# Cosine attention and a highway layer on one core: k of three batches and x of the last one transposed by DMA, another end for the last two tiles

## The chip, the cores and the metric

The kernel runs on one core of one Trainium2 chip. The metric is the device time of one execution in microseconds (us); several executions are timed and the median is given. A profile is one more execution, recorded by the hardware profiler: it has a time of its own, and a span from the first to the last instruction of the program. The engines are TensorE (PE; its weight loads are PEld), VectorE (DVE), ScalarE (ACT), GpSimd (POOL) and SyncE (SP). Each runs its own queue of instructions in order and waits for others on semaphores.

## The reference

```
q, k, v: (8, 12, 448, 64) float32;  tau = 0.1;  w_h, w_t: (768, 768);  b_t: (768)

q_n = q / (norm(q, axis=-1) + 1e-6);   k_n = k / (norm(k, axis=-1) + 1e-6)
attn = softmax(q_n @ k_n.T / tau)                      # per batch and head, 448 x 448
x = (attn @ v), heads side by side                     # (8 * 448, 768)

H = maximum(x @ w_h, 0)
T = 1 / (1 + exp(-(x @ w_t + b_t)))
out = T * H + (1 - T) * x                              # (3584, 768) float32
```

## The kernel before

The eight batches go through three parts: normalising and transposing q and k, attention, and the highway layer (the code calls it ffn). The parts of several batches overlap in time. Twelve heads make six pairs, and two pairs make a group, so each batch has three groups g. A sequence of 448 is split into 64 rows l of 7 columns j. A q or k tile has two halves of 64 partitions, one for the even and one for the odd heads; an x tile has two such halves for two neighbouring columns j.

*Normalising.* `norm` squares a group of q or k (`sq`, on ScalarE; L377) and VectorE sums it (`rd`, L385). `newton` on VectorE makes the inverse root y for batches 1 to 7; `lnexp` on ScalarE does it for batch 0. `scale` multiplies by y into the fp16 tiles qn and kn (L425), on GpSimd but for a part of batch 0. kn has eight columns: seven and one that a shift leaves half empty and that is set to zero.

*Transposing.* `turn` makes qT and kT. On TensorE that is seven or eight transposes against an identity (L442) into PSUM, and a copy by VectorE (`cpq`, `cpk`; L450). For q of batches 3 to 7 (QDMA) it is one transposing DMA from SyncE's queue instead (`xd7`, L444). x of batches 1 to 6 (XDMA) goes the same way (`xd6`, and `xd3` for the short last tile of a batch; L648); x of batches 0 and 7 by TensorE (`xt6`, `xt3`; L644) and a copy (`cpx`, L654).

*Attention.* Scores are products of K = 64 in the two row halves of the array at once (`qk`, L484; `qkt`, L495), ScalarE makes their exponentials (L490, L497), products with v follow (`av`, L509 and L514; `avt`, in column halves, L522), and VectorE divides by the sums (`rc`, `ev`; L529, L530) into x.

*The highway layer.* A batch has four tiles, numbered 4 b + i: three of 768 columns and a short one of 384 (i = 3). So tiles 28 to 31 are those of the last batch. A tile's product with w_t (wi = 0) and with w_h (wi = 1) comes in halves of 384 columns, each issued as two groups of three products (L668). The short tile's go in pairs to the two column halves of the array (L665). After w_t: z = P + bias (`za`, DVE, L677), tanh on ScalarE (`th`, L684), T = 0.5 tanh + 0.5 (`gt`, DVE, L686). After w_h: hm = max(P, 0) - x (`hm`, DVE, L680), hm = T * hm (`gg`, DVE, L689), os = x + hm (`out`, on GpSimd; on VectorE for tiles 30 and 31, L694). Two DMAs from SyncE's queue store the two partition halves (`st`; L701 for short tiles, L704 for the others).

What sets the order of everything: each operation is recorded with what it reads and writes, and ORDER, a list written into the kernel, gives the order in which they are issued, SLOTS which buffer of its ring each one takes (eight banks of PSUM, three kn, four kT, four os and so on). An operation whose name is in PORT keeps GpSimd's next such instruction behind the VectorE one that is recorded ahead of it. Wherever the array changes between whole (F), two row halves (T) and two column halves (C), the operations' mode changes.

Around the change, q's transposing DMA stands in `turn` like this:

```
if nm == "q" and b in QDMA:
    op("SP", f"xd7 {b} {g}", lambda: nc.sync.dma_start(
        R("qT", i)..., R("qn", i)..., transpose=True), r=[("qn", i, 0), ("qn", i, 1)], w=[tn(nm, i)])
    return
```

Of the kernel before, what the change touches and what calls it, by code (L numbers as in the profile page):

```python
# [12 lines left out]
ALU = mybir.AluOpType  # L13
# [78 lines left out]
""".split()  # L92
)

SLOTS = {
    "qr": "01010101",
    "kr": "0120121",
    "kn": "012012012012102021210210",
    "vr": "01001010",
    "vp": "01010101",  # L100
    "sq": "012012012120120120120121201201012210210122202101",
    "n2": "01010101",
    "y": "01201201",
    "tu": "01010101010",
# [93 lines left out]
def kernel(  # L198
# [11 lines left out]
    nc = tc.nc  # L210
# [3 lines left out]
    CC = DM // 128  # L214
# [591 lines left out]
```

## Time and profile before

| | |
|---|---|
| median of 3 runs | 257.26 us (257.17 to 257.95) |
| profiled execution | 256.1 us, span 254.3 us |
| granted TensorE clock, mean | 0.968 |
| busy: PE, DVE, ACT, POOL | 236.7, 210.6, 214.6, 170.2 us |
| DMA queue q1 (SyncE's), share of the 16 engines | 51.7% |
| DMA queue q0 (GpSimd's), share of the 16 engines | 36.7% |

A busy time is the time in which an engine had an instruction under way. TensorE's products overlap, so their pace is read from the distance between starts. In a group's line the part ahead of the bar names the line of the program, the engine, the operation, its tiles and shapes and the count; behind it stand the busy time, the mean of one in ns, the idle time just before such instructions, and what ended it. In the chain of the work that ended last, each line has a start, a length and what ran.

### The profile page before, as it was taken

Reading aid. Unit: us, or ns where it says so; the run is one execution under the profiler, and the core shown is the slowest. Engines: PE = TensorE matmul, PEld = TensorE weight load, DVE = VectorE, ACT = ScalarE, POOL = GpSimd, SP = SyncE. Lnnn points to the kernel's source line nnn. Section 1 sums busy time; section 2 is a strip of 40 time slices with the busy share of each in tenths; the row PEclk is TensorE's granted clock in tenths of the full one; section 3 lists DMA queues with packets and bytes.
Section 4 is the critical chain, followed back from the end, with each engine's and each line's share of the span. In section 5 each row is a group of like instructions: output and inputs, shape, how many; then the busy total and the mean of one; then the engine's idle time right before and its main releaser. Section 6 shows DMA issues by size and latency. Waiting matters only on the chain.

```text
span 254.3 us, 7465 instructions
## 1 busy us (share of the span) xinstructions
PE 236.7 (93%) x2937; PEld 150.3 (59%) x2937; DVE 210.6 (83%) x471; ACT 214.6 (84%) x425; POOL 170.2 (67%) x210
## 2 busy tenths in 40 slices
PE   8376999999999999999999999999999999999980
PEld 2156776566656675566575665656556755667640
DVE  4887797897999999989997789989986763868893
ACT  2688999999999999999999999999968997591210
POOL 5478366956978696689879965687737784142440
PEclk9756999999999999999999999999999999999998
DMA  7999999999599995899999999995792065407175
GB/s 225 284 223 207 270 266 239 146 145 292 81 141 327 177 148 110 167 296 169 185 144 198 307 159 153 163 342 108 146 214 65 3 136 107 129 0 189 22 213 139
DMA packets 63283, 44.72 MB, mean 176 GB/s; under 512 B 38928, under 2 KB 60048, under 8 KB 63248
## 3 DMA queue, kind: packets, MB, share of 16 engines
q1 hardware_dynamic: 43120, 31.11, 51.7%
q0 software_dynamic: 19856, 12.68, 36.7%
q8 instruction: 23, 0.38, 0.6%
q10 hardware_dynamic: 272, 0.46, 0.5%
q14 instruction: 12, 0.10, 0.1%
HBM read 38.34 MB, written 11.01 MB: 194 GB/s over the span
## 4 chain that ended last, share of the span: by engine, by line
PE 78%; ACT 9%; DVE 5%; DMA 3%; POOL 1%; issue 1%; SPq 0%; DVEq 0%; ACTq 0%
PE B L668 34%; PE B L484 11%; PE B L514 9%; PE B L665 5%; PE B L442 5%; PE B L509 4%; ACT E L490 3%; DMA qr<-in_q_dram 3%; PE B L522 3%; PE B L495 3%; ACT sq L377 3%; ACT E L574 2%; PE B L561 2%; PE B L588 1%; POOL kn L425 1%
## 5 line engine op out<-in xcount | busy, mean ns | idle before, releaser
L490 ACT ACTIVATE E<-B 128x448 f16<-128x448 f32 x252 | 125.2, 640 | 7.5 <-PE B L484 6.7
L668 PEld LDWEIGHTS <-xT 128*128 128x128 f16 x576 | 52.6, 98 | 37.9 <-issue 6.7
L694 POOL TENSOR_TENSOR os<-x,hm 128x384 f32<-128x384 f16 x53 | 47.5, 917 | 30.0 <-DVE hm L689 23.6
L425 POOL TENSOR_TENSOR qn<-qr,y 128x448 f16<-128x448 f32 x47 | 43.2, 932 | 26.1 <-DVE qn L425 5.7
L668 PE MATMUL B<-wh,xT 128*128 128x384 f16 x288 | 57.0, 326 | 0.1
L668 PE MATMUL B<-wt,xT 128*128 128x384 f16 x288 | 55.6, 326 | 0.1
L385 DVE TENSOR_REDUCE n<-sq 128x14 f32<-128x896 f32 (+1 forms) x50 | 51.1, 1037 | 1.8 <-ACT sq L377 1.8
L425 POOL TENSOR_TENSOR kn<-kr,y 128x448 f16<-128x448 f16 x42 | 39.0, 943 | 7.8 <-DVE vp L456 3.9
L684 ACT ACTIVATE tt<-z 128x768 f16<-128x768 f32 (+1 forms) x32 | 25.8, 835 | 17.3 <-DVE z L677 17.3
L514 PE MATMUL B<-vp,E 128*128 128x65 f16 x756 | 37.6, 193 | 0.0
L484 PE MATMUL B<-qT,kT 64*128 64x448 f16 x252 | 35.1, 353 | 0.1
L514 PEld LDWEIGHTS <-E 128*128 128x128 f16 x756 | 33.4, 97 | 2.3
L677 DVE TENSOR_TENSOR z<-B,bias 128x384 f32<-128x384 f32 x48 | 25.5, 550 | 10.1 <-PE B L668 9.0
L680 DVE SCALAR_TENSOR_TENSOR hm<-B,x 128x384 f16<-128x384 f32 x56 | 30.2, 548 | 3.0 <-PE B L668 1.7
L509 PE MATMUL B<-vp,Et 128*128 128x130 f16 x126 | 28.1, 223 | 0.0
L497 ACT ACTIVATE Et<-B 128x448 f16<-128x448 f32 x42 | 26.8, 650 | 0.4
L530 DVE SCALAR_TENSOR_TENSOR x<-B,rd 128x448 f16<-128x448 f32 x42 | 25.6, 616 | 0.7
L377 ACT ACTIVATE sq<-qr 128x896 f32<-128x896 f32 (+1 forms) x24 | 24.5, 1036 | 0.6 <-DMA qr<-in_q_dram 0.6
L377 ACT ACTIVATE sq<-kr 128x896 f32<-128x896 f16 x21 | 22.2, 1075 | 0.8 <-DMA kr<-in_k_dram 0.8
L335 POOL DMA_DIRECT2D vr<-in_v_dram x32 | 21.7, 683 | 0.7 <-DVE vp L456 0.7
L574 ACT ACTIVATE E<-B 128x384 f16<-128x384 f32 (+1 forms) x42 | 21.3, 636 | 0.9 <-PE B L561 0.6
L450 DVE COPY kT<-B 128x1024 f16<-128x1024 f16 x23 | 15.7, 681 | 4.0 <-PE B L442 2.0
(72 smaller groups left out, 305.2 us busy)
## 6 DMA issues: line engine op xcount, KB each, us to landing
out_dram<-os SPq DMA_DIRECT2D x48, 192.0 KB, 3.3
qr<-in_q_dram SPq DMA_DIRECT2D x6, 1344.0 KB, 8.5
kr<-in_k_dram POOLq DMA_DIRECT2D x7, 672.0 KB, 9.9
vr<-in_v_dram POOLq DMA_DIRECT2D x16, 192.0 KB, 8.0
qr<-in_q_dram SPq DMA_DIRECT2D x6, 448.0 KB, 7.4
vr<-in_v_dram POOLq DMA_DIRECT2D x16, 144.0 KB, 6.4
out_dram<-os SPq DMA_DIRECT2D x16, 96.0 KB, 3.4
wt<-in_moe_w_t_dram POOLq DMA_DIRECT2D x1, 1152.0 KB, 13.2
```

The source lines that it names most:

```text
L377: nc.scalar.activation(dst, src, AF.Square, scale=sc)
L385: nc.vector.reduce_sum(R("n2", b)[:, c : c + 7 * n], a, axis=AX.X)
L425: ENG[eng].tensor_mul(R(nm + "n", i)[:, o : o + NJ, t, :], source(nm, b, g)[:, t].rearrange("l (j d) -> l j d", d=D), R("y", b)[:, c : c + ...
L484: nc.tensor.matmul(R("B", ("S", n, c, t))[:, 0:S], lhsT=R("kT", i)[ln, s, 128 * c : 128 * c + 128], rhs=queries(ln), start=True, stop=True)
L490: nc.scalar.activation(R("E", n)[:, at : at + 7, :].rearrange("l j x -> l (j x)"), R("B", ("S", n, c, t))[:, 0:S], AF.Exp)
L497: op("ACT", f"expt {n}", lambda: nc.scalar.activation(R("Et", n).rearrange("l j x -> l (j x)"), R("B", ("St", n))[:, 0:S], AF.Exp), r=[("B ...
L509: nc.tensor.matmul(U[:, 2 * c : 2 * c + 2, :], lhsT=Et[:, 2 * c : 2 * c + 2, :].rearrange("l j x -> l (j x)"), rhs=vp[:, 6:8, 0:65], start ...
L514: nc.tensor.matmul(U[:, 2 * c + t, :], lhsT=E[:, at : at + 2, :].rearrange("l j x -> l (j x)"), rhs=vp[:, 3 * t + m, 0:65], start=False, s ...
L574: op("ACT", f"ex{m} {n}", lambda X=X, m=m, t=t, o=o: nc.scalar.activation(flat()[:, o + 512 * t : o + 512 * t + m], R("B", X)[:, 0:m], AF. ...
L668: nc.tensor.matmul(P[:, 0:MH], lhsT=xT[:, cc, :], rhs=w_[:, cc, MH * mh : MH * mh + MH], start=(cc == 0), stop=(cc == CC - 1))
L680: op("DVE", f"hm {g} {mh}", lambda at=at, sl=sl, mh=mh: nc.vector.scalar_tensor_tensor(out=R("hm", g)[:, sl], in0=R("B", at)[:, 0:MH], sca ...
L694: op(eng, f"out {g} {mh}", lambda sl=sl, mh=mh: ENG[eng].tensor_add(R("os", g)[:, sl], xpart(mh), R("hm", g)[:, sl]), r=[("gg", g), xk], w ...
```

## The change

k of batches 5 to 7 (KDMA) is transposed by two DMAs for each group, one for each half of the partitions, from SyncE's queue (`xdk`). So that their blocks land in order, kn is laid out with every other column, each scaling of k becomes two instructions (four and three columns; `kn4`, `kn3`), and the loads and copies of v follow the same order of columns. x of batch 7 is transposed by DMA as well. The squares of k, group 1, of batches 2 to 5 (SQP) move from ScalarE to GpSimd.

The last two tiles (30 and 31; NLATE) are combined in another form. With T known, VectorE makes `cx`: os = (T - 1) * x. Behind each product with w_h come two operations: `hg`: hm = max(P, 0) * T, and `ou`: os = hm - os. For tile 31 the product with w_h goes in two halves of 192 columns to each column half of the array (`fth`), with its `hg3` and `ou3`. The two stores of these tiles go one from SyncE's queue and one from ScalarE's (`sl6`, `sl3`).

ORDER and SLOTS are written anew throughout.

```diff
-    XDMA, QDMA = range(1, B - 1), range(3, B)
+    XDMA, QDMA, KDMA = range(1, B), range(3, B), range(5, B)
+    SQP = tuple(("k", b, 1) for b in range(2, 6))
...
-        engs = SPLIT.get(i, (("DVE" if i in SQV else "ACT"),))
+        engs = SPLIT.get(i, (("DVE" if i in SQV else "POOL" if i in SQP else "ACT"),))
...
+                elif eng == "POOL":
+                    nc.gpsimd.tensor_mul(dst, src, src)
...
     def scale(nm, b, g, engs):
+            for lo, hi in ((0, 7),) if nm == "q" else ((0, 4 - t), (4 - t, 7)):
...
+                        N[:, :, t, :] if nm == "q" else N[:, lo > 0 : (lo > 0) + 2 * (hi - lo) - 1 : 2, t, :],
...
+        if nm == "k" and b in KDMA:
+            for s in range(2):
+                op("SP", f"xdk {b} {g} {s}", lambda s=s: nc.sync.dma_start(
+                    R("kT", i)[:, s, :].rearrange("p (j x) -> p j x", j=8),
+                    R("kn", i)[64 * s : 64 * s + 64].rearrange("l j t d -> l (j t d)"), transpose=True),
+                   r=[("kn", i, 0), ("kn", i, 1), ("zkn",)], w=[tn(nm, i)])
+            return
...
+        late, last = g >= 4 * B - NLATE, g == 4 * B - 1
...
+                if last and wi:
+                    for n in range(2):
...
+                                    c0 = MH * h + MH // 2 * n
+                                    nc.tensor.matmul(P[64 * h : 64 * h + 64, 0 : MH // 2], lhsT=xT[:, cc % 3, 64 * (cc // 3) : 64 * (cc // 3) + 64],
+                                                     rhs=w_[:, cc, c0 : c0 + MH // 2], start=(cc == 0), stop=(cc == CC - 1))
+                        op("PE", f"fth {g} {n}", half, r=[("xT", g), (wn,)], w=[("B", at)], mode="C")
...
+                        op("DVE", f"hg3 {g} {n}", ...scalar=0.0, in1=R("tt", g)[:, sl], op0=ALU.max, op1=ALU.mult),
+                        op("DVE", f"ou3 {g} {n}", ...nc.vector.tensor_sub(R("os", g)[:, sl], R("hm", g)[:, sl], R("os", g)[:, sl]),
...
+                elif late:
+                    op("DVE", f"hg6 {g} {mh}", ...
+                    op("DVE", f"ou6 {g} {mh}", ...
...
+                        op("DVE", f"cx {g} {n}", ...
+                            out=R("os", g)[:, sl], in0=R("tt", g)[:, sl], scalar=-1.0, in1=xpart(n), op0=ALU.add, op1=ALU.mult),
...
+        if late:
+            for h in range(2):
...
+                    eng = (nc.sync, nc.scalar)[h]
...
+                op(("SP", "ACT")[h], f"sl{nb} {g} {h}", put, r=[("os", g)], w=[("o", g, h)])
+            return
```

More of the change, by code (lines that the diff above doesn't have):

```diff
@@ L97 @@
     "kr": "0120121",
-    "kn": "012012012012102021210210",
-    "vr": "01001010",
+    "kn": "012012012012021021021012",
+    "vr": "01010101",
     "vp": "01010101",
-    "sq": "012012012120120120120121201201012210210122202101",
+    "sq": "012012010101201201201201021021021021201021102102",
     "n2": "01010101",
@@ L104 @@
     "tu": "01010101010",
-    "qn": "012012012012021201210210",
-    "qT": "01230123012301230123012",
-    "kT": "01230123013201320132013",
-    "E": "012010201201021010210210120120210210120120210210102102120",
-    "Et": "012102102101201210210210210201012021021210",
-    "rd": "010101010011010101010101010010101101010101010101010101",
-    "x": "012012012",
-    "xT": "01234012340213402310423014230412",
-    "z": "01101010100110010101101001000101",
-    "tt": "01101010011010101010101101101010",
@@ L115 @@
-    "hm": "01202012021201202001212021021021",
-    "os": "01230321203231013013021231203203",
-    "B": (
-        "0123456701234567012345671203614352007630156421653024160426350160234156043217654306512307641275463170"
-        "2546124367012537251057634274637201437062453061546271345062746107346072436571407534605271237605471653"
-        "7401236752413051742035674235106754602713052614702673147635213502460321745027453721430672415360716025"
-        "4137621407125674305407625137052467235603715263056173546025170435170674021573620417023641536071357260"
-        "4137462607143561253047216032761043540261573163025743674567234627154360714635703612465143670135740126"
-        "0371564301324725706354016713402613527041052361703214065324710"
+    "qn": "012012022102021021021021",
@@ new lines @@
+    "qT": "01230123102102312032103",
+    "kT": "01230123012301230123012",
+    "E": "012012021021021222012012021021201201201201201012020102102",
+    "Et": "012102102102102101210212102012102101210210",
+    "rd": "011011010101101010100101010101010101010101010101010101",
+    "x": "012012012",
+    "xT": "01234021342014302130410234210421",
+    "z": "01011001011010001000010110101010",
+    "tt": "01010110101010101010101110001010",
+    "hm": "01220210021020120210012001200120",
+    "os": "01231023123023110310310120310312",
@@ new lines @@
+    "B": (
+        "0123456701234567012345670213467061532462153476240157632570624153027162504327142657302716034152467102"
+        "4720634173254176403576415260432560142357160257460271506432051643125076314203762041374631206340517513"
+        "7062451034761520461752473105632046715647120531620451745612034572067153047125671230751671045276342510"
+        "7364203643571640745127364072534126526317431720657124035617204637156243574023157413054267126012735607"
+        "1243726410746513240175026731426036752314057126540372612075163471760542310521705632147627305641203675"
+        "2106312745603217561437021547502631407263517420631"
@@ L124 @@
     ),
 }
-PORT = ("nt", "gt", "gg", "vc", "qn", "kn", "vt", "out")
+PORT = ("nt", "gt", "gg", "vc", "qn", "kn", "vt", "out", "cx", "ou")
 class Op:
@@ L216 @@
     NC, NJ = 3, 7
-    WARM, NF = 18, 0
-    XDMA, QDMA = range(1, B - 1), range(3, B)
+    WARM, NF, NLATE = 18, 0, 2
+    XDMA, QDMA, KDMA = range(1, B), range(3, B), range(5, B)
     GROUPS = ((0, 1), (1, 2), (2, 3)), ((0, 1), (1, 3)), ((0, 3),)
@@ L293 @@
     for i, t in enumerate(TILES["kn"]):
-        op("DVE", f"zkn {i}", zero("DVE", [(t[:, 0, 1, :], 0.0), (t[:, 7, 0, :], 0.0)]), w=[("zkn",)])
+        op("DVE", f"zkn {i}", zero("DVE", [(t[:, 6, 1, :], 0.0), (t[:, 7, 0, :], 0.0)]), w=[("zkn",)])
     op("DVE", "zw", zero("DVE", [(wz[:, :], 0.0), (eps[:, :], 1e-14)]), w=[("wz",), ("eps",)])
@@ L333, in fn @@
             def fn(t=t, jj=jj, j0=j0, n=n):
-                c = 64 if (t, jj) == (0, 1) else 0
-                nc.gpsimd.dma_start(R("vr", b)[64 * jj : 64 * jj + 64, 6 * t : 6 * t + 6, c : c + 64 * n].rearrange("l h (c d) -> l h c d", c=n),
+                nc.gpsimd.dma_start(R("vr", b)[64 * jj : 64 * jj + 64, 6 * t : 6 * t + 6, 0 : 64 * n].rearrange("l h (c d) -> l h c d", c=n),
                                     v_src(b)[:, 6 * t : 6 * t + 6, j0 : j0 + n, :])
@@ L377, in fn @@
                     nc.scalar.activation(dst, src, AF.Square, scale=sc)
+                elif eng == "POOL":
+                    assert sc == 1.0
+                    nc.gpsimd.tensor_mul(dst, src, src)
                 else:
@@ L421, in scale, with fn @@
         for t, eng in enumerate(engs):
-            def fn(t=t, eng=eng):
-                c = col(nm, g) + 7 * t
-                o = t if nm == "k" else 0
-                ENG[eng].tensor_mul(
-                    R(nm + "n", i)[:, o : o + NJ, t, :],
-                    source(nm, b, g)[:, t].rearrange("l (j d) -> l j d", d=D),
-                    R("y", b)[:, c : c + 7].unsqueeze(2).to_broadcast([128, NJ, D]))
-            op(eng, f"{nm}n {b} {g} {t}", fn, r=[token(nm, b, g), ("y", b, nm, g)], w=[(nm + "n", i, t)])
+            for lo, hi in ((0, 7),) if nm == "q" else ((0, 4 - t), (4 - t, 7)):
+                def fn(t=t, eng=eng, lo=lo, hi=hi):
+                    c = col(nm, g) + 7 * t
+                    N = R(nm + "n", i)
+                    ENG[eng].tensor_mul(
+                        N[:, :, t, :] if nm == "q" else N[:, lo > 0 : (lo > 0) + 2 * (hi - lo) - 1 : 2, t, :],
+                        source(nm, b, g)[:, t, 64 * lo : 64 * hi].rearrange("l (j d) -> l j d", d=D),
+                        R("y", b)[:, c + lo : c + hi].unsqueeze(2).to_broadcast([128, hi - lo, D]))
+                op(eng, f"{nm}n{hi - lo} {b} {g} {t}", fn, r=[token(nm, b, g), ("y", b, nm, g)], w=[(nm + "n", i, t)])
     def turn(nm, b, g):
@@ L439, in fn @@
             for j in range(nj):
-                to = j if nm == "q" else 2 * ((j - 1) % 3) + (j - 1) // 3 if 0 < j < 7 else 6 + (j == 7)
-                nc.tensor.transpose(T[:, to], R(nm + "n", i)[:, j].rearrange("l t d -> l (t d)"), ident[:, :])
+                nc.tensor.transpose(T[:, j], R(nm + "n", i)[:, j].rearrange("l t d -> l (t d)"), ident[:, :])
         if nm == "q" and b in QDMA:
@@ L457, in fn @@
                     R("vp", b)[:, p0:p1, 3 * t : 3 * t + 3, 0:D],
-                    R("vr", b)[:, 6 * t + p0 : 6 * t + p1, 64 - 64 * t : 256 - 64 * t].rearrange("l p (c d) -> l p c d", c=NC))
+                    R("vr", b)[:, 6 * t + p0 : 6 * t + p1, 0:192].rearrange("l p (c d) -> l p c d", c=NC))
             op("DVE", f"vc{p1 - p0} {b} {p0} {t}", fn, r=[("vr", b, t, 0), ("vr", b, t, 1), ("zvp",)],
@@ L465, in fn @@
                 ln = slice(64 * t, 64 * t + 64)
-                ENG[eng].tensor_copy(R("vp", b)[ln, :, 6 + t, 0:D], R("vr", b)[ln, 6 * t : 6 * t + 6, 192 * t : 192 * t + 64])
+                ENG[eng].tensor_copy(R("vp", b)[ln, :, 6 + t, 0:D], R("vr", b)[ln, 6 * t : 6 * t + 6, 192:256])
             op(eng, f"vt {b} {t}", fn, r=[("vr", b, t, t), ("zvp",)], w=[("vp", b, 6)])
@@ L669, in mm, with half @@
                                              start=(cc == 0), stop=(cc == CC - 1))
+                if last and wi:
+                    for n in range(2):
+                        at = ("P", g, wi, n)
+                        def half(n=n, at=at, w_=w_):
+                            P, xT = R("B", at), R("xT", g)
+                            for cc in range(CC):
+                                for h in range(2):
[3 more added lines that the diff above has]
+                        op("PE", f"fth {g} {n}", half, r=[("xT", g), (wn,)], w=[("B", at)], mode="C")
+                        sl = slice(MH // 2 * n, MH // 2 * n + MH // 2)
+                        op("DVE", f"hg3 {g} {n}", lambda at=at, sl=sl: nc.vector.scalar_tensor_tensor(
+                            out=R("hm", g)[:, sl], in0=R("B", at)[:, 0 : MH // 2], scalar=0.0, in1=R("tt", g)[:, sl], op0=ALU.max, op1=ALU.mult),
+                           r=[("B", at), ("gt", g)], w=[("hm", g, n)], u=[("tt", g)])
+                        op("DVE", f"ou3 {g} {n}", lambda sl=sl: nc.vector.tensor_sub(R("os", g)[:, sl], R("hm", g)[:, sl], R("os", g)[:, sl]),
+                           r=[("hm", g, n), ("cx", g)], w=[("os", g)], u=[("hm", g)])
+                    continue
                 for lo in (0, 3):
@@ L678, in ffn @@
                         R("z", g)[:, sl], R("B", at)[:, 0:MH], biast[:, :] if tail else bias[:, sl]), r=[("B", at), ("b",)], w=[("z", g)])
+                elif late:
+                    op("DVE", f"hg6 {g} {mh}", lambda at=at, sl=sl: nc.vector.scalar_tensor_tensor(
+                        out=R("hm", g)[:, sl], in0=R("B", at)[:, 0:MH], scalar=0.0, in1=R("tt", g)[:, sl], op0=ALU.max, op1=ALU.mult),
+                       r=[("B", at), ("gt", g)], w=[("hm", g, mh)], u=[("tt", g)])
+                    op("DVE", f"ou6 {g} {mh}", lambda sl=sl: nc.vector.tensor_sub(R("os", g)[:, sl], R("hm", g)[:, sl], R("os", g)[:, sl]),
+                       r=[("hm", g, mh), ("cx", g)], w=[("os", g)], u=[("hm", g)])
                 else:
@@ L688, in ffn, with put @@
                    r=[("tt", g)], w=[("gt", g)], u=[("tt", g)])
+                if late:
+                    for n in range(nb // 3):
+                        sl = slice(MH * n, MH * n + MH)
+                        op("DVE", f"cx {g} {n}", lambda sl=sl, n=n: nc.vector.scalar_tensor_tensor(
+                            out=R("os", g)[:, sl], in0=R("tt", g)[:, sl], scalar=-1.0, in1=xpart(n), op0=ALU.add, op1=ALU.mult),
+                           r=[("gt", g), xk], w=[("cx", g)], u=[("tt", g), ("os", g)])
+        if late:
+            for h in range(2):
+                def put(h=h):
+                    rows, O = out[b * S : b * S + S].rearrange("(l j) m -> j l m", j=NJ), R("os", g)[64 * h : 64 * h + 64]
+                    eng = (nc.sync, nc.scalar)[h]
+                    if tail:
+                        eng.dma_start(rows[6, :, MH * h : MH * h + MH], O[:, 0:MH])
+                    else:
+                        eng.dma_start(rows[2 * i + h], O[:, :])
+                op(("SP", "ACT")[h], f"sl{nb} {g} {h}", put, r=[("os", g)], w=[("o", g, h)])
+            return
         op("DVE", f"gg{nb} {g}", lambda: nc.vector.tensor_mul(R("hm", g)[:, 0:W], R("tt", g)[:, 0:W], R("hm", g)[:, 0:W]),
            r=[("gt", g), ("hm", g)], w=[("gg", g)], u=[("tt", g), ("hm", g)])
-        eng = "DVE" if b == B - 1 and i >= 2 else "POOL"
+        eng = "DVE" if g >= 4 * B - 2 else "POOL"
         for mh in range(1 if tail else 2):
```

144 rows, old and new, of the table ORDER are left out of this document.

## The prediction

> **What bounds the kernel now.** I read the page first, then stretches of time, then the chain that ended last, then single groups. Page, busy time and chain by engine:
>
> ```profile
> span 254.3 us, 7465 instructions
> PE 236.7 (93%) x2937; PEld 150.3 (59%) x2937; DVE 210.6 (83%) x471; ACT 214.6 (84%) x425; POOL 170.2 (67%) x210
> PE 78%; ACT 9%; DVE 5%; DMA 3%; POOL 1%; issue 1%; SPq 0%; DVEq 0%; ACTq 0%
> ```
>
> TensorE leads, but a busy TensorE is not one at its peak, so I ask each stage who is idle:
>
> ```profile
> core 0: us, PE busy (x) PEld busy (x) DVE busy (x) ACT busy (x) POOL busy (x), PEclk, DMA share, GB/s
> 0.00:20.00 20.00, 12.62 (x77) 6.87 (x78) 15.00 (x35) 12.50 (x23) 12.06 (x21) 0.74 1.04 244
> 40.00:60.00 20.00, 19.53 (x275) 11.81 (x272) 18.24 (x42) 20.00 (x41) 14.45 (x19) 1.00 1.13 191
> 160.00:180.00 20.00, 20.00 (x279) 12.73 (x273) 17.71 (x41) 19.44 (x39) 14.13 (x17) 1.00 1.01 196
> 180.00:200.00 20.00, 20.00 (x234) 12.21 (x234) 16.01 (x39) 16.59 (x36) 12.71 (x16) 1.00 0.55 126
> 241.50:254.30 12.80, 5.50 (x46) 3.13 (x43) 8.50 (x17) 1.36 (x2) 3.17 (x4) 0.90 0.68 176
> 28.00:247.00 219.00, 218.22 (x2761) 138.26 (x2759) 186.41 (x415) 194.46 (x390) 152.75 (x183) 1.00 0.88 168
> ```
>
> There are three stages. Up to 28 us data are still arriving and TensorE has holes. From 28 to 247 us it is busy in 218.22 of 219 us. From 247 us it has nothing left, and VectorE and the stores finish. ScalarE has no idle time from 40 to 60 us either, so it stands close behind. The pace inside the middle stage is in the chain (start, length, what):
>
> ```profile
> 107.98 0.45 PE B L442 x8
> 123.52 0.67 PE B L484 x6
> 124.19 1.08 PE B L668 x6
> 125.72 0.97 PE B L668 x6
> 219.90 0.19 PE B L484 x2
> 232.39 0.84 PE B L644 x15
> 233.22 8.30 PE B L668 x51
> ```
>
> Fifty-one products at L668 in 8.30 us are 0.163 us each, back to back: this stage has no wait to remove, only work. Work taken from TensorE here shortens the end one for one, if nothing new makes it wait. One more price stands here: six score products (three pairs) would need 3 x 0.19 = 0.57 us and take 0.67, and the six L668 products behind them take 1.08 us where others take 0.97. Each change of the array's shape (whole, two row halves, two column halves) costs 0.10 us.
>
> **The change, part by part.**
>
> *k of batches 5 to 7.* Nine groups lose eight transposes each on TensorE: 9 x 0.45 = 4.05 us, all in the middle stage. VectorE loses their nine copies. SyncE gains 18 transposing DMAs of half the partitions each. The rows:
>
> ```profile
> L450 DVE COPY kT<-B 128x1024 f16<-128x1024 f16 x23 | 15.7, 681 | 4.0 <-PE B L442 2.0 <-PE B L567 1.5 <-ACT E L490 0.5
> L648 SPq DMA_TRANSPOSE xT<-x x24: 1206/1242/2117, 67.9 to 210.5; - x24
>   PEld L668: 0.9, 3
> DMA to landing us min/median/max: 2.3/2.8/9.8
> L444 SPq DMA_TRANSPOSE qT<-qn x15: 1221/1233/1585, 88.6 to 213.8; - x15
> DMA to landing us min/median/max: 2.9/4.1/7.2
> ```
>
> The nine copies are 9 x 0.68 = 6.1 us of VectorE, worth nothing here because it isn't the bound. A transposing DMA holds SyncE's queue 1.24 us, so the 18, with four new ones for x, hold it 22 x 1.24 = 27 us more. Each waits there for both halves of its normalised k from GpSimd, and stores, x and q transposes stand behind it. What hides the landing is distance: I added up, at the paces of this trace, the TensorE work that the new order puts between the last of a group's three DMAs (two k, one q) and the first product that reads them. For the nine groups it is 6.8, 6.4, 8.9, 5.6, 7.0, 4.3, 8.2, 5.7 and 6.1 us. A landing of 4.1 us (the median of the q rows, nearest in source and size) fits under all nine, so I take 0. The bounds are 0 and, with the slowest q landing of 7.2 us in every group, 0.4 + 0.8 + 1.6 + 0.2 + 2.9 + 1.5 + 1.1 = 8.5 us lost.
>
> *x of the last batch.* 15 transposes take 0.84 us, so 21 take 1.18 us, all on TensorE's path. In their place the first DMA must land before tile 28 starts.
>
> ```profile
> L529 DVE RECIPROCAL rd<-B 128x7 f32<-128x7 f32 x42 | 8.3, 200 | 8.3 <-PE B L522 4.9 <-PE B L514 1.7 <-ACT Et L497 1.3
> L530 DVE SCALAR_TENSOR_TENSOR x<-B,rd 128x448 f16<-128x448 f32 x42 | 25.6, 616 | 0.7
> ```
>
> Behind the last attention product the new order holds ten half-groups of three products or pairs, 10 x 3 x 0.163 = 4.9 us. Reciprocal and division take 0.2 + 0.6 us of it, and x lands 2.8 us after its issue: 3.6 against 4.9. So 0; without that cover it costs up to 2.8 us once. The second tile is needed 3.4 us after the first and issued 1.24 us later.
>
> *Changes of shape.* Counted in the order of TensorE's instructions: 163 before, 172 after; 9 x 0.10 = +0.9 us.
>
> *The end.* Rows of the last microseconds and of VectorE's prices:
>
> ```profile
> 245.85 1.14 PE L665 MATMUL B<-wh,xT 128*64 128x384 f16 x12
> 247.56 1.02 DVE L694 TENSOR_TENSOR os<-x,hm 128x384 f32<-128x384 f16 x2
> 248.96 0.25 DVE L686 TENSOR_SCALAR tt<-tt 128x384 f16<-128x384 f16 x1
> 249.64 0.56 DVE L694 TENSOR_TENSOR os<-x,hm 128x384 f32<-128x384 f16 x1
> 250.22 1.11 SPq L701 DMA_DIRECT2D out_dram<-os  x2
> L595 DVE SCALAR_TENSOR_TENSOR x<-B,rd 128x256 f16<-128x256 f32 x9 | 3.6, 417 | 0.1
> L617 DVE SCALAR_TENSOR_TENSOR x<-B,rd 128x128 f16<-128x128 f32 x3 | 0.8, 288 | 0.1
> L689 DVE TENSOR_TENSOR hm<-tt,hm x32: 342/549/809, 53.0 to 249.2; 128x768 f16<-128x768 f16 x24, 128x384 f16<-128x384 f16 x8
> ```
>
> Before: products end at 246.99, VectorE at 250.20, 3.2 us later; it is VectorE's backlog that ends last, not a dependence. After: behind tile 30's last products stand only two halves of tile 31, together as long as the twelve at L665 (six pairs, 6 x 0.163 = 0.98 us). So 0.98 us ahead of the last product's end tile 30 is done, and from there VectorE has hg6, ou6, gt3, ou6, hg3, cx, hg3, ou3, ou3. A 384-wide one follows the next at 0.47 us (two in 1.02), gt3 takes 0.25, and a 192-wide one, between 288 and 417 ns, follows at some 0.3. Sum: 4 x 0.47 + 0.25 + 4 x 0.3 + 0.05 for the last one's end = 3.4, so 2.4 us behind the last product. GpSimd's two adds of tile 29 run beside this. In this trace such a VectorE product took 549 ns at the median and 809 at most, so I add 0.3: 2.7, a gain of 0.5 us (bounds: 0.95, if there is no backlog, and 3.2, as now: a gain of 2.2 or 0). The Trainium skill, "SBUF — State Buffer", section "Who interferes with whom", would have an operation with two SBUF inputs blocked for the whole of GpSimd's; that is one add of 0.9 us, 0.6 more than I take, and the sum below would be -4.4.
>
> The stores: two issues on one queue take 1.11 us; on two queues one goes beside the other, so 0.55 us less (bounds 0 and 0.6; 0 if the two transfers follow each other). End: -0.5 - 0.55 = -1.05. The Trainium skill, "DMA: Bandwidth & Descriptors", section "Rules for kernel authors", advises against two transfers to disjoint partition halves, from two engines as well, because they serialise. By it the second queue brings nothing, and the sum would be -4.45; no run so far shows two such stores from two queues.
>
> *Squares and splits.* Four squares of k move from ScalarE to GpSimd, and each scaling of k there becomes two instructions:
>
> ```profile
> L377 ACT ACTIVATE sq<-kr 128x896 f32<-128x896 f16 x21 | 22.2, 1075 | 0.8 <-DMA kr<-in_k_dram 0.8
> L425 POOL TENSOR_TENSOR kn<-kr,y 128x448 f16<-128x448 f16 x42 | 39.0, 943 | 7.8 <-DVE vp L456 3.9 <-DVE y L403 2.4 <-DVE rd L616 0.6
> L694 POOL TENSOR_TENSOR os<-x,hm 128x384 f32<-128x384 f16 x53 | 47.5, 917 | 30.0 <-DVE hm L689 23.6 <-DVE hm L680 2.9 <-DMA out_dram<-os 1.7
> L787 POOL MEMSET const-float32-0.0<- 128x1 f32 x1 | 0.1, 98 | 0.2 <-issue 0.2
> ```
>
> ScalarE loses 4 x 1.08 = 4.3 us, which it needs to lose: it has no idle time to keep up with a shorter TensorE. GpSimd gains 4 x 2 x 0.94 = 7.5 us and 47 more instructions at about 0.1 (an almost empty one takes 98 ns), 4.7 us; its idle time of 30.0 us ahead of the adds alone covers both. Cost 0; if GpSimd were late, k would be, and that is the late rival below.
>
> *The opening.* GpSimd now issues two loads of v and the whole of wt ahead of its first product, and that product stands behind a second scaling on VectorE.
>
> ```profile
> vr<-in_v_dram POOLq DMA_DIRECT2D x16, 192.0 KB, 8.0
> vr<-in_v_dram POOLq DMA_DIRECT2D x16, 144.0 KB, 6.4
> wt<-in_moe_w_t_dram POOLq DMA_DIRECT2D x1, 1152.0 KB, 13.2
> ```
>
> I take +0.4, an estimate: half of one of the 0.94 us scalings. The bounds are 0 and 3 us: 144 + 1152 + 192 KB at 244 GB/s are 6.1 us of traffic, half of which may fall on the third group's q and k.
>
> Sum: -4.05 - 1.18 + 0.9 - 1.05 + 0.4 = -5.0 us. Profiled execution: 256.1 us with a span of 254.3; it becomes 251.1 with a span of 249.3. The median of the runs, 257.26, stands 1.16 above the profiled one; I forecast 252.3.
>
> **The rivals.**
>
> *k lands late* (slower). Place: the products at L484 that open batches 5 to 7's groups. For it: up to 180 us the DMA engines are full (share 1.01 at 160 to 180), transposes landed after up to 9.8 us, and SyncE's queue gets longer. Against: TensorE lost 0.9 us to all 24 transposes of x, and beyond 180 us the share is 0.55. At 7.2 us in every group it loses 8.5 us: 252.3 + 8.5 = 260.8. It eats the gain up from about 6.6 us per landing (0.2 + 1.0 + 2.3 + 0.9 + 0.5 = 4.9 us lost).
>
> *ScalarE sets the pace.* For it: 20.00 of 20 us. Then what k frees before 180 us (six groups, 2.7 us) turns into waits for exponentials: 255.0. Against: it loses 4.3 us itself, and has 3.4 us free in the stretch from 180 us.
>
> *The opening costs more.* At 3 us instead of 0.4: 254.9. For it: DMA share 1.04 there; against: TensorE has other groups' work to turn to.
>
> **How the numbers follow.** Forecast 0.62, late k 0.15, opening 0.13, ScalarE 0.10. Measurement can tell 0.3%, 0.8 us, from no change: faster means below 256.5, slower above 258.0. The forecast's own range is 250 (no backlog at the end) to 254 (x of the last batch uncovered). The range of all runs from 249.5, where the opening's holes shrink as well, to 257.0, which takes in both mild rivals and a small part of late k. Faster: nearly all of the forecast (0.61) and most of the mild rivals (0.18), 0.79. Slower: most of late k, 0.14. Same: 0.07.
>
> **What would show it.** Right: TensorE without holes from 28 us to its last product at about 242.5; no wait for transposed k over 0.3 us; six L668 products still in 0.97 us; the last VectorE operation some 2.7 us behind the last product, and two stores issued side by side. Wrong: weight loads of k waiting on transposing DMAs by several us in all, holes before L484 with ScalarE full, or batch 0 ending over 2 us behind its new place in the order.

## The result and the profile after

The changed kernel takes 258.33 us (median of 14 runs, 256.84 to 260.65) and the kernel before, beside it, 257.09 us: a ratio of 1.0052 (95% interval 1.0031 to 1.0074). It is slower by half a per cent; 252.3 us had been forecast, and 257.0 us was the upper end of the range. The profiled execution takes 258.85 us with a span of 257.1 us, against 256.1 and 254.3 us before. Ratios here and below leave out every execution more than 1.5% above its kernel's fastest and medians don't, so the two differ where executions scatter (e1, with 5 of 12 left out, and e7, with 8 of 12).

From the page of the changed kernel, its span, busy times and chain:

```profile
span 257.1 us, 7374 instructions
PE 232.9 (91%) x2856; PEld 145.8 (57%) x2856; DVE 206.2 (80%) x462; ACT 211.9 (82%) x421; POOL 184.4 (72%) x261
PE 48%; DMA 11%; ACT 7%; DVE 6%; SPq 6%; POOL 5%; issue 3%; DVEq 0%; POOLq 0%
```

TensorE is busy 3.8 us less (236.7 us before), yet its share of the chain fell from 78% to 48%; DMA and SyncE's queue (SPq) came in. Where the time went is read by stretches (start and end, length, TensorE's busy time with its count, granted clock, DMA share, GB/s). First before, then after, each up to TensorE's last product at 246.99 and 250.25 us:

```profile
core 0: us, PE busy (x), PEclk, DMA share, GB/s
0.00:28.00 28.00, 18.46 (x177) 0.76 1.06 239
28.00:40.00 12.00, 11.86 (x198) 1.00 1.13 270
40.00:247.00 207.00, 206.36 (x2569) 1.00 0.87 163
```

```profile
0.00:28.00 28.00, 17.85 (x153) 0.76 1.08 255
28.00:40.00 12.00, 11.28 (x177) 0.86 1.15 262
40.00:78.00 38.00, 37.41 (x542) 1.00 0.98 163
78.00:84.00 6.00, 3.43 (x28) 1.00 1.57 126
84.00:104.00 20.00, 19.88 (x271) 1.00 0.96 259
104.00:110.00 6.00, 5.66 (x89) 1.00 1.24 162
110.00:204.00 94.00, 93.98 (x1163) 1.00 1.04 177
204.00:212.00 8.00, 5.16 (x41) 1.00 0.80 131
212.00:250.25 38.25, 38.25 (x410) 1.00 0.65 150
```

Length less busy time is the hole. Up to 28 us, to 40 us and behind that it is, before: 9.54 + 0.14 + 0.63 = 10.3 us. After: 10.15 + 0.72 + 6.5 = 17.4 us, of which 2.57 us lie at 78 to 84 us and 2.84 us at 204 to 212 us. So TensorE ends 7.1 - 3.8 = 3.3 us later, and from its last product to the end of the span it is 6.85 us instead of 7.3.

The two large holes in the chain of waits of the changed kernel (start, length, what), with GpSimd's row from the timeline of the first:

```profile
74.70 0.19 PE B L525 x6
74.91 6.17 DMA xT<-x
81.12 0.66 PE B L681 x3
```

```profile
75.50 2.81 POOL L336 DMA_DIRECT2D vr<-in_v_dram  x4
```

```profile
193.45 1.64 SPq L454
195.13 2.62 SPq L454
...
203.05 2.57 SPq L454
205.67 5.33 DMA qT<-qn
211.13 0.55 PE B L495 x4
```

At 81 us the first products of tile 4 wait for its x. Before, SyncE issued that transpose as the first of batch 1's four; the new order has it third, behind tiles 5 and 7. It lands 6.17 us after its issue, and from 0.6 us after that issue on GpSimd sends off four loads of v (75.50 to 78.31 us). At 211 us the scores of batch 7's second group wait for q. Its transposing DMA (L448) stands behind four halves of k (L454) on SyncE's queue, two of which held the queue 2.6 us each instead of 1.24; the queue has no gap from 193.45 to 205.67 us, and then q takes another 5.33 us to land.

The end, in the timeline of the changed kernel:

```profile
248.62 1.78 POOL L751 TENSOR_TENSOR os<-x,hm 128x384 f32<-128x384 f16 x2 [2.22 <-DVE os L732]
249.06 1.18 PE L694 MATMUL B<-wh,xT 128*64 128x192 f16 x24
249.81 1.01 DVE L716 TENSOR_TENSOR os<-hm,os 128x384 f32<-128x384 f16 x1
250.91 0.55 DVE L716 TENSOR_TENSOR os<-hm,os 128x384 f32<-128x384 f16 x1
252.48 0.61 DVE L701 TENSOR_TENSOR os<-hm,os 128x192 f32<-128x192 f16 x2
253.12 0.47 SPq L741 DMA_DIRECT2D out_dram<-os  x1
253.13 0.50 ACTq L741 DMA_DIRECT2D out_dram<-os  x1
```

VectorE ends at 253.10, 2.85 us behind the last product (3.2 before; 2.7 forecast). The two stores do go side by side, but from VectorE's end to the span's end it is still 4.0 us (4.1 before).

### The profile page after: what moved, and what is told of

It is laid out like the page before. It is cut to its first block, busy times and chain, and to the rows that moved or that the text cites. A ratio compares the mean times of both kernels' runs of the same rounds, so it can differ in the third digit from the quotient of the medians.

```text
span 257.1 us, 7374 instructions
## 1 busy us (share of the span) xinstructions
PE 232.9 (91%) x2856; PEld 145.8 (57%) x2856; DVE 206.2 (80%) x462; ACT 211.9 (82%) x421; POOL 184.4 (72%) x261
## 4 chain that ended last, share of the span: by engine, by line
PE 48%; DMA 11%; ACT 7%; DVE 6%; SPq 6%; POOL 5%; issue 3%; DVEq 0%; POOLq 0%
PE B L681 22%; PE B L495 7%; PE B L525 5%; ACT E L501 5%; DMA xT<-x 5%; SPq L454 4%; PE B L678 3%; DMA qr<-in_q_dram 3%; PE B L446 2%; PE B L520 2%; POOL kn L431 2%; DMA qT<-qn 2%; PE B L506 2%; PE B L533 2%; DMA out_dram<-os 2%
## 5 line engine op out<-in xcount | busy, mean ns | idle before, releaser
L681 PEld LDWEIGHTS <-xT 128*128 128x128 f16 x576 | 51.9, 98 | 40.9 <-issue 7.6
L751 POOL TENSOR_TENSOR os<-x,hm 128x384 f32<-128x384 f16 x53 | 48.1, 916 | 32.4 <-DVE hm L746 7.9
L681 PE MATMUL B<-wt,xT 128*128 128x384 f16 x288 | 56.7, 326 | 3.0 <-DMA xT<-x 2.9
L431 POOL TENSOR_TENSOR kn<-kr,y 128x256 f16<-128x256 f16 (+1 forms) x84 | 45.9, 565 | 5.8 <-DVE y L408 3.6
L719 DVE SCALAR_TENSOR_TENSOR hm<-B,x 128x384 f16<-128x384 f32 x53 | 28.8, 550 | 11.3 <-PE B L681 7.0
L710 DVE TENSOR_TENSOR z<-B,bias 128x384 f32<-128x384 f32 x48 | 25.6, 549 | 12.4 <-PE B L681 10.8
L508 ACT ACTIVATE Et<-B 128x448 f16<-128x448 f32 x42 | 25.6, 628 | 1.2 <-PE B L506 1.1
L585 ACT ACTIVATE E<-B 128x512 f16<-128x512 f32 (+1 forms) x42 | 19.8, 553 | 0.3
L495 PEld LDWEIGHTS <-kT 64*128 64x128 f16 x252 | 8.7, 94 | 16.3 <-issue 12.5
L379 ACT ACTIVATE sq<-kr 128x896 f32<-128x896 f16 x17 | 17.0, 1016 | 0.4 <-DMA kr<-in_k_dram 0.4
## 6 DMA issues: line engine op xcount, KB each, us to landing
wt<-in_moe_w_t_dram POOLq DMA_DIRECT2D x1, 1152.0 KB, 23.8
```

Source lines behind the costliest of these rows:

```text
L379: nc.scalar.activation(dst, src, AF.Square, scale=sc)
L431: ENG[eng].tensor_mul(N[:, :, t, :] if nm == "q" else N[:, lo > 0 : (lo > 0) + 2 * (hi - lo) - 1 : 2, t, :], source(nm, b, g)[:, t, 64 * l ...
L495: nc.tensor.matmul(R("B", ("S", n, c, t))[:, 0:S], lhsT=R("kT", i)[ln, s, 128 * c : 128 * c + 128], rhs=queries(ln), start=True, stop=True)
L508: op("ACT", f"expt {n}", lambda: nc.scalar.activation(R("Et", n).rearrange("l j x -> l (j x)"), R("B", ("St", n))[:, 0:S], AF.Exp), r=[("B ...
L681: nc.tensor.matmul(P[:, 0:MH], lhsT=xT[:, cc, :], rhs=w_[:, cc, MH * mh : MH * mh + MH], start=(cc == 0), stop=(cc == CC - 1))
L719: op("DVE", f"hm {g} {mh}", lambda at=at, sl=sl, mh=mh: nc.vector.scalar_tensor_tensor(out=R("hm", g)[:, sl], in0=R("B", at)[:, 0:MH], sca ...
```

## The experiments

Theory A: the change takes off TensorE what it was meant to, and the time is given back as waits in queues, at three places that can be mended by order alone: the opening's loads, tile 4's x, and q of batch 7. Theory B: something else, such as ScalarE's pace, late k as such, or the new operations themselves, costs the time, and moving transfers brings little.

| | edit | median, us | ratio to before (95%) |
|---|---|---|---|
| e1 | opening's loads back | 257.05 | 0.9950 (0.9916 to 0.9984) |
| e2 | SyncE's order, first try | 260.95 | 1.0140 (1.0106 to 1.0174) |
| e3 | e1 and e2 | 259.76 | 1.0099 (1.0069 to 1.0128) |
| e5 | e1, SyncE's order, second try | 253.92 | 0.9838 (0.9808 to 0.9869) |
| e9 | e5's SyncE order alone | 254.83 | 0.9911 (0.9877 to 0.9944) |
| e12 | tile 4's x alone | 255.27 | 0.9905 (0.9871 to 0.9939) |
| e10 | e5, load of q 7 earlier | 258.46 | 1.0062 (1.0028 to 1.0096) |
| e4 | k back on TensorE | 263.68 | 1.0280 (1.0237 to 1.0324) |
| e8 | squares of k back on ScalarE | 265.14 | 1.0285 (1.0251 to 1.0319) |
| e6 | before, with the new end | 258.34 | 1.0053 (1.0031 to 1.0075) |
| e7 | last four stores on one queue | 259.11 | 0.9998 (0.9956 to 1.0040) |
| e11 | e5, with the old end | 252.75 | 0.9834 (0.9803 to 0.9865) |

All but e6 start from the changed kernel. In the diffs an operation stands by its name in the order; ld is a load.

**e1, the opening's loads.**

```diff
 GpSimd: ldv4 0 0 0,
-ldv3 0 0 1, ldwt, ldv4 1 0 0, qn7 0 0 1, kn3 0 0 1, kn4 0 0 1,
+qn7 0 0 1, kn3 0 0 1, kn4 0 0 1, ldv3 0 0 1,
 kn4 0 1 1, ..., qn7 0 1 0,
-ldwh,
+ldwt,
 ..., kn4 0 2 0,
+ldwh, ldv4 1 0 0,
```

> The changed kernel, but on GpSimd's queue the loads of the opening stand where they stood before the change: the fourth load of v behind the first scalings, wt behind group 1's, wh and the first load of v of batch 1 behind group 2's. Nothing else moves. Theory A (the lost time is waits at three places in queues; the opening is one of them, because wt and v take DMA time from q and k): TensorE's waits up to 40 us fall from 12.0 to about 9 us, so 258.3 becomes about 255.3 us. Theory B (the new order of the opening itself costs it, or the DMA engines are overfull as a whole so that another transfer is late instead): within 1 us of 258.3.

Faster than the changed kernel by 1.0% by the ratios and by 0.5% by the medians, a part of what A expected (255.3 us). In the changed kernel ScalarE waited for a q load of batch 1 (engine, line, what for: us in total, times, longest):

```profile
ACT sq L379 <- DMA qr<-in_q_dram: 1.8, 1, 1.8
```

That wait is gone in e1, and TensorE's busy time in the first 28 us rose from 17.85 to 19.47 us; wt landed 12.4 us after its issue instead of 23.8 (13.2 before). TensorE's holes up to 40 us are 8.6 to 8.9 us in e1 and the four other kernels with this opening (e3, e5, e10, e11); they are 10.9 us in the changed kernel and 9.6 to 11.3 us in the six others that keep its opening. But the wait at tile 4 is there in e1's profiled execution of 258.61 us (4.27 us busy from 78 to 84 us), and the runs lie scattered from 254.2 to 260.1 us.

**e2 and e3, SyncE's order, first try.**

```diff
 SyncE, batch 1:   ldq 3 0,
-xd6 5, xd3 7, xd6 4, xd6 6
+xd6 4, xd6 5, xd3 7, xd6 6
 SyncE, batch 7:   st 19,
-xd3 23, xd7 7 0, xdk 7 1 1, xdk 7 1 0, xd7 7 1, xd6 24
+xd7 7 0, xd7 7 1, xdk 7 1 1, xdk 7 1 0, xd3 23, xd6 24
```

> The changed kernel, with three DMAs moved on SyncE's queue alone: tile 4's x transpose goes first of batch 1's instead of third, q of group 1 of batch 7 goes ahead of that group's two k transposes, and tile 23's x goes behind them. Theory A (waits in a queue that is in the wrong order): the waits of 2.7 us ahead of tile 4 and of 2.6 us ahead of batch 7's group 1 shrink to under 0.5 us each, 258.3 becomes about 254 us. Theory B (the DMA engines are overfull): what is moved back is late instead, or the same first products still wait; within 1 us of 258.3.

> Both moves together. Theory A: the gains add up, about 251 us, and TensorE has under 11 us of waits in all. Theory B: not under 257 us.

Both are slower than the changed kernel: a miss. The wait at tile 4 has gone (6.00 of 6 us busy from 78 to 84 us in both), but to let q pass I had moved the x of tile 23 (xd3 23) back, and this became the next wait. From e3's chain, then TensorE over its last piece (busy, then clock), then the same 24 products in e12's chain:

```profile
201.41 3.41 DMA xT<-x
204.86 3.82 PE B L672 x24
```

```profile
204.86:208.68 3.82, 3.82 (x26) 0.55 1.09 179
```

```profile
201.44 1.95 PE B L672 x24
```

In e3 TensorE waited 3.7 us there, its granted clock was 0.55 behind the wait (1.00 from 196 to 201 us), and the 24 products took 3.82 us instead of 1.95. In e2 it is the same place, with a wait of 7.1 us, but its profiled execution took 267.14 us, 6 us above the median of its runs.

**e5, e9 and e12: second try, and its parts.** Now a store is moved behind instead of an x; e9 has SyncE's part of e5 alone, e12 only its first line.

```diff
 SyncE, batch 1:
-xd6 5, xd3 7, xd6 4, xd6 6
+xd6 5, xd6 4, xd3 7, xd6 6
 SyncE, batch 7:   xdk 7 0 0,
-st 19, xd3 23, xd7 7 0, xdk 7 1 1, xdk 7 1 0, xd7 7 1, xd6 24
+xd3 23, xd7 7 0, xd7 7 1, xdk 7 1 1, xdk 7 1 0, st 19, xd6 24
```

> The changed kernel with the opening's loads moved back as in the first experiment, and another order on SyncE's queue: tile 4's x transpose second of batch 1's instead of third; in batch 7 the q transpose of group 1 ahead of that group's two of k, with tile 23's x kept where it was and only the store of tile 19 moved behind them. Theory A (the waits come from the order in which the queue issues, so they go if nothing that is needed sooner is moved back): the waits of 2.7 us at tile 4 and of 2.6 us at batch 7's group 1 shrink to under 0.7 us each, no new one over 1 us appears, and the time is some 4 us under that of the loads alone: about 252.5 us. Theory B (the DMA engines are overfull; whatever is last in a row of transposes is late): not under 256 us, with a wait of over 2 us at another place.

> Only SyncE's row is changed against the changed kernel (tile 4's x transposed second of batch 1, the q of batch 7's second group ahead of its k, one store moved behind that k); the opening's loads stay as the change put them. Theory A (two separate queue losses that add): the changed kernel's 258.3 less what SyncE's row is worth, 4.4 us of e5_fixed less 1.3 us of e1_loads = 3.1 us: 255.2 us, with no wait over 0.5 us at tile 4's first products (81 us) and at batch 7's second group (211 us), and 12 us of holes before 40 us as in the changed kernel. Theory B (one loss, the opening's, from which the later ones follow): 257.5 us or more, the waits at 81 and 211 us still there.

> The changed kernel with one transfer moved: tile 4's x is transposed second of batch 1 on SyncE, not third. Theory A (the wait of 2.7 us at 81 us is that one landing, 6.2 us in the third place against 2.4 in the second, and independent of batch 7's): 258.3 - 2.7 = 255.6 us, with no wait over 0.5 us at tile 4's first products and the wait of some 2.6 us at 211 us still there. Theory B (whichever x stands third is late by the same, or TensorE's lead is eaten by the next thing that comes late): 257.5 us or more, with a new wait of 1 to 3 us between 81 and 110 us.

The times are near those of theory A: 253.92, 254.83 and 255.27 us, where 252.5, 255.2 and 255.6 had been expected, and in none of the three does TensorE have a hole at tile 4. e12 moves one DMA by one place and gains 3.1 us on the changed kernel (255.27 against 258.33; 2.7 us had been expected). TensorE's stretches from 78 to 84 and from 204 to 212 us in e12, and the landings of batch 1's four x transposes (smallest, median, largest), first in the changed kernel, then in e12:

```profile
78.00:84.00 6.00, 6.00 (x65) 1.00 1.29 174
204.00:212.00 8.00, 6.85 (x44) 1.00 0.98 201
```

```profile
DMA to landing us min/median/max: 2.4/4.5/8.4
```

```profile
DMA to landing us min/median/max: 2.8/3.6/7.1
```

The hole at tile 4 has gone, though the fourth transpose still lands after 7.1 us: nothing needs it so soon. Whether the loads of v or the place in the row made tile 4's landing long isn't separated, since no run moves those loads alone. The second half of theory A is weaker. The hole from 204 to 212 us is 2.84 us in the changed kernel's profile, but 1.31 us in e7, which is the same kernel up to there, and 0.60 and 1.15 us in e1 and e12, which leave batch 7's row as it was. With q moved as well it is 1.11 (e9) and 1.32 us (e5); e9 and e12 can't be told apart in time. What waits there in e12 is an x (1.2 us), not q. So A's expectation for e12 was wrong on this point, and q's own place on the queue isn't shown to cost time. The opening's loads, added to e9, bring another 0.7% (e5).

**e10, the next wait removed.** A's "no new one over 1 us appears" fails in e5's profile: ScalarE waits 3.2 us, and then TensorE, for the load of batch 7's q:

```profile
159.30 9.59 DMA qr<-in_q_dram
```

```diff
 SyncE:
-st 9, xd6 18, xd6 17, xd3 19, xd6 16, ldq 7 0, xdk 6 0 0
+ldq 7 0, st 9, xd6 18, xd6 17, xd3 19, xd6 16, xdk 6 0 0
```

> e5_fixed with one more move: the load of batch 7's q is issued on SyncE ahead of the four x transposes of batch 4 instead of behind them, some 7 us earlier. Theory A (the rest of the loss is the landing of that load, 9.6 us behind an issue at 159.3 us, for which ScalarE's squares waited 3.2 us and TensorE 2.1 us): 252.0 us, no wait for that load, PE's last product 2 us earlier against e5_fixed. Theory B (the DMA engines are full from 158 to 172 us, so that another landing becomes late in its place: a k transpose of batch 6 or the x of batch 4): 253.9 us, as e5_fixed, with a new wait of 1 to 2 us between 158 and 180 us.

Slower than e5 by 4.5 us: B, and more of it than B expected. From e10's chain:

```profile
150.53 1.67 PE B L672 x18
152.48 8.32 DMA xT<-x
160.85 2.10 PE B L675 x6
```

Issued 1.7 us behind the load, the first of the four x transposes now takes 8.32 us, and TensorE's products wait 4.2 us for it; in e5 the same four landed after 3.6 to 4.6 us. Where the load stood in e5, its profiled execution lost 2.4 us (TensorE busy in 1.57 us of the 4 from 168 to 172 us). But that execution took 256.38 us, 2.5 above e5's median, and e11, whose order is e5's up to the end, has no hole there (8.00 of the 8 us from 165 to 173 us, against 5.52 in e5). So the wait that e10 was to remove was not one of every execution, while the load in front of the transposes costs 4.5 us.

**e4, k back on TensorE**, the transposes and copies some 4 us ahead of the first product that reads them.

```diff
-    XDMA, QDMA, KDMA = range(1, B), range(3, B), range(5, B)
+    XDMA, QDMA, KDMA = range(1, B), range(3, B), range(0)
```

> The changed kernel with k of batches 5 to 7 back on TensorE: eight transposes for each of nine groups some 4 us ahead of the group's first product and a copy by VectorE, no transposing DMA of k. The halved scalings on GpSimd stay. Theory A: TensorE's work grows by 4.05 us, and of the waits only the 2.6 us in batch 7 goes; about +1.5 us, 259.8. Theory B (k's transposes overfill the DMA engines and SyncE's queue everywhere behind 130 us): the waits that go outweigh the work, 256 us or less.

```profile
PE 238.7 (91%) x2928; PEld 150.2 (57%) x2928; DVE 210.7 (80%) x471; ACT 212.5 (81%) x421; POOL 184.3 (70%) x261
```

5.35 us slower than the changed kernel, and neither theory expected it (259.8 us, or 256 and less). TensorE's busy time says the same: 238.7 against 232.9 us, 72 products more. That is 0.64 us for each of the nine groups, where the prediction had 0.45. The row of k's transposes alone accounts for 5.5 us, first in the changed kernel, then in e4:

```profile
L446 PE MATMUL B<-ident,kn 128*128 128x128 f16 x120 | 10.6, 237 | 0.8 <-POOL kn L431 0.5 <-DVE kn L431 0.2
L440 PE MATMUL B<-ident,kn 128*128 128x128 f16 x192 | 16.1, 230 | 1.3 <-POOL kn L425 0.8 <-DVE kn L425 0.5
```

Products overlap, so a part of such a row's time can be shared with its neighbours; e4 also has three more changes of shape than the changed kernel, 0.3 us. How the difference to 0.45 splits isn't settled. The wait in batch 7 did go (8.00 of 8 us busy from 204 to 212 us), but from 110 to 204 us there are 2.07 us of holes instead of 0.02. k by DMA is the part that pays.

**e8, the squares of k back on ScalarE.**

```diff
-    SQP = tuple(("k", b, 1) for b in range(2, 6))
+    SQP = ()
```

> The changed kernel with the four squares of k back on ScalarE, in the same places of the order. If ScalarE sets the pace between 40 and 130 us, 4 x 1.08 us come back as waits of TensorE ahead of the exponentials' banks: about 262 us. If TensorE is the bound there and ScalarE only close behind, under 1 us: 258.3 to 259.3. If GpSimd's 1.7 us squares were what delayed q, k and the adds, it is faster, 257 or less.

6.8 us slower than the changed kernel. From its chain:

```profile
70.70 1.66 ACT sq L373 x2
72.36 1.75 ACT E L495 x4
...
76.98 8.58 DMA xT<-x
85.60 0.80 PE B L675 x3
```

A square of k (1.09 us) now stands on ScalarE ahead of exponentials that batch 1's x needs. The transposes of x begin at 74.28 us instead of 72.24, together with GpSimd's four loads of v instead of ahead of them, and tile 4's takes 8.58 us. TensorE is busy 8.93 us of the 14 from 78 to 92. So ScalarE has no reserve there, as the prediction said. How the 6.8 us split between its pace and the late transposes isn't shown: in the profiles the hole from 78 to 92 us, at tile 4, is 5.07 instead of 2.57 us, and the holes from 40 to 78 and from 92 to 120 us, away from it, are 3.7 instead of 1.1 us together.

**e6, e7 and e11: the end.** e6 puts the new end (NLATE, `cx`, `hg`, `ou`, `fth`, two queues) into the kernel before and nothing else. e7 takes ScalarE's queue out of it:

```diff
-                    eng = (nc.sync, nc.scalar)[h]
+                    eng = nc.sync
```

e11 is e5 with the old end: three operations behind each product, `out` for tiles 30 and 31 on VectorE, tile 31 in two groups of 384 columns, all stores from SyncE.

> The kernel before with the new end alone: tiles 30 and 31 by the two operations behind their products, tile 31 in halves, its products with w_t ahead of tile 30's last, stores on two queues; everything up to there as before. By the prediction's sum for the end (-0.5 for VectorE's backlog, -0.55 for the stores) 256.0 us against 257.0. If two stores that go side by side follow each other in the DMA engines, the second term is 0: 256.5.

> The changed kernel with all four of the last stores issued from SyncE's queue, as before the change; nothing else moves. If two queues save one issue (0.55 us), this takes 258.9 against 258.3 us. If the two stores serialise behind the issue, it takes 258.3, within 0.3 us, and the time from the last VectorE operation to the end stays near 4.0 us.

> e5_fixed with the kernel before's end (tiles 30 and 31 with VectorE's usual three operations behind their products, both column halves of tile 31 as before, whole-tile stores from SyncE alone). The prediction's price of the new end (1.05 us): 254.9 us. By the traces (new end 0.35 us less backlog, stores 0.1 us less): 254.4 us. If the new end is worth nothing or costs, as when it was put into the kernel before by itself (e6_tail, 1.0 us slower): 253.0 to 253.9 us; the last VectorE operation then ends 3.2 us behind the last product, and the program 4.1 us behind that.

e6 is 1.0 us slower than before, against a forecast gain: VectorE ends 4.1 us behind the last product instead of 3.2. e7 can't be told from the changed kernel in time, with runs from 254.7 to 262.0 us and overlapping intervals, but the profiles answer the question on the stores: from VectorE's end to the end of the span it is 3.8 us in e7 (252.67 to 256.5), 3.9 in e11 and 4.1 before, all on one queue, and 4.0, 4.1 and 4.2 us in the changed kernel, e5 and e6 on two. e11 has the shortest time of all. Its end:

```profile
243.50 1.14 PE L670 MATMUL B<-wh,xT 128*64 128x384 f16 x12
246.63 0.56 DVE L699 TENSOR_TENSOR os<-x,hm 128x384 f32<-128x384 f16 x1
247.32 1.18 SPq L706 DMA_DIRECT2D out_dram<-os  x2
```

VectorE ends 2.55 us behind the last product (244.64) and the span 6.5 us behind it; with the new end it was 6.8 in e5 and 6.85 in the changed kernel. In ratio e11 and e5 are alike, so the new end is worth nothing that can be measured, and by these single profiles it costs 0.3 us.

## Why the prediction was wrong, by its own steps

**k, the landing "0".** As far as it went, this was right: no row of the changed kernel has TensorE waiting for a transposed k. In the median the 18 DMAs held the queue (1.27 us) and landed (4.0 us) as forecast:

```profile
L454 SPq DMA_TRANSPOSE kT<-kn x18: 1194/1266/2616, 139.0 to 215.6; - x18
DMA to landing us min/median/max: 2.7/4.0/7.9
```

The step that failed is what was counted. The prediction says of SyncE's longer queue that "stores, x and q transposes stand behind it", and prices that at nothing: the lead is worked out for the nine groups of k and for tile 28, and for none of the other transposes whose place on the queue the new order changes. Its signs of being wrong name k's weight loads, the exponentials and batch 0, not x or q. Tile 4's x went from first to third of its batch and lost 2.6 us; e12 shows that this one place decided between slower and faster. For batch 7's second group I had a lead of 5.7 us from the issue of q, and took the issue as given; in the changed kernel q, not k, came last there, and TensorE stood 2.84 us in that profile. That hole differs between executions of the same order (1.31 us in e7), and its cause stays open.

**k, the work.** Right in direction and too small: 4.05 us, or 4.35 with e4's three changes of shape, against 5.4 to 5.8 us (e4).

**x of the last batch.** Right: from 212 us to the last product TensorE has no hole (38.25 of 38.25 us).

**The opening, "+0.4".** Too small. The holes up to 40 us grew by 1.2 us, and moving the loads back brought 1.3 us by the medians (e1 against the changed kernel). From 28 to 40 us the granted clock was 0.86 instead of 1.00, but e7 and e12, which have the same opening, show 1.00 and 0.72 in that stretch, so what the clock cost isn't shown. The bound of 3 us, the rival, isn't reached by what is shown.

**The end.** The backlog of 2.7 us was nearly right (2.85), but the old end, put behind e5's order, has 2.55 (e11): what the end gained comes from the order ahead of it, and nothing from the new operations. `ou6` beside GpSimd's adds took 1.01 us and alone 0.55, the 0.46 us shown in the timeline above; I had allowed 0.3. The Trainium skill, "SBUF — State Buffer", section "Who interferes with whom", has such an operation wait out GpSimd's: by that it would end 0.55 us behind the second add, at 250.95 us (an estimate). It ended at 250.82, so the trace agrees within 0.13 us. The stores, "-0.55": wrong. The Trainium skill, "DMA: Bandwidth & Descriptors", section "Rules for kernel authors", says of transfers to disjoint partition halves that they serialise, from two engines as well. The runs agree that the second queue brings nothing: 4.0 us on two queues, 3.8 on one.

**ScalarE and GpSimd.** The relief of ScalarE was needed (e8), and GpSimd had room: 184.4 us busy against 170.2, and TensorE's products waited 0.5 us in all for its scalings of k. With the order mended, ScalarE's share of the chain rises from 7% to 20% (e12) and 22% (e5), so it may well be the next bound.

With the order mended, e5 and e11 come to 0.984 of the time before, about 253 us. That this is near the forecast is partly luck, because k's work brought 1.3 us or more beyond its term and the end 1.05 us less. The sum was wrong above all in pricing the order at nothing: by the medians tile 4's x (3.1 us, e12) and the opening's loads (1.3 us, e1) make 4.4 of the 6.0 us between forecast and result, and e5, which mends both, gains 4.4 us.

The range that the prediction gives for the forecast itself, 250 to 254, doesn't follow from its own bounds: no backlog at the end gives about 250.5, and x of the last batch uncovered by 2.8 us gives 255.1.

## What to carry to other kernels

When a change rewrites the order, list every transfer whose place on its queue moved, not only those that the change adds, and work out for each how long after its issue it is first needed and which bulk loads start in between. Here transposing DMAs of x landed in 2.4 to 2.8 us ahead of the loads and in 6 to 9 us beside them; put the one that is needed first ahead of the loads, and give up the place of a store, not of another operand, for it. Before mending a wait that one profile shows, look whether a second execution has it, and what the move puts behind the moved load.

## What the runs showed of the hardware

Three things I had not expected. Landing times of transposing DMAs went with what was issued beside them: 2.4 to 2.8 us for the first ones of batch 1, 6.17 and 8.4 us for those that GpSimd's four loads of v joined, 8.58 in e8 where the loads came first, 8.32 in e10 behind a load of q (3.6 to 4.6 us in e5 with that load behind them). SyncE's queue itself was held 2.6 us instead of 1.24 by some of the half transposes. And a longer stop of TensorE was paid twice: behind the 3.7 us in e3 the granted clock was 0.55 and 24 products took 3.82 us instead of 1.95, and behind the 4.2 us in e10 the clock was 0.62 (160.8 to 165 us), while behind the changed kernel's stops of 2.6 and 2.4 us it was 1.00 (81 to 85 and 211.1 to 215 us).
